# A linear-attention and MLP kernel on one core: row tables made by turning, four stages at once from stage 12 on, and a program listed anew

## The chip, the core and the metric

The kernel runs on one core of a Trainium2 chip. A core has a matrix engine (TensorE, "PE" in the profile), two elementwise engines that read its result banks (VectorE, "DVE", and ScalarE, "ACT"), a general engine (GpSimd, "POOL") and a queue engine (SyncE, "SP"). Each engine takes its instructions in order; they wait for each other through semaphores. The metric is device time in microseconds for one launch, the median of several runs; lower is better.

## What is computed

For 4 batches and 8 heads, 768 tokens of 48 channels each, a decayed linear attention is run along the tokens; its output, 3072 rows of 384, goes through an MLP of 384 to 2048 to 384 with a leaky ReLU:

```python
for t in range(S):
    kt, vt, rt = (k[:, :, t].copy(), v[:, :, t].copy(), r[:, :, t].copy())
    cur = np.einsum('bhd,bhe->bhde', u[None] * kt, vt)
    y[:, :, t] = np.einsum('bhd,bhde->bhe', rt, state + cur)
    state = w[None, :, :, None] * state + np.einsum('bhd,bhe->bhde', kt, vt)
...
h = x @ w_in
g = np.maximum(0.01 * h, h)
return (g @ w_out).astype(np.float32)
```

Inputs and output are fp32 in device memory; the kernel works in bf16 with fp32 accumulation.

## The kernel before

**Stages.** The tokens are cut into 24 stages of 128 tokens of one batch (stage n is batch n mod 4, chunk n div 4), so stage n takes the state that stage n - 4 left. A stage consists of steps, each with a letter in the program:

- `k`, `r`, `v` (`load_one`, L224): three loads, issued by Pool, each 128 x 384, turned to bf16 on the way.
- `P` (`prep_half`, L373, DVE): r times a table of w to the power t, and k times a table of w to the power -t. The tables are the row tables `qtab` and `ktab` (tokens along partitions, channels along a row).
- Turning, so that channels lie along partitions: `T` on PE with a copy `t` on ACT or DVE for stages 0 to 5, `X` (L378) as a DMA transpose on SP's queue from stage 6 on. Stage 0 is turned raw and multiplied with a table that is already turned (`turned`, made by `E`, L337, from w laid along partitions).
- `A` (L465, PE): the 128 x 128 score tiles of eight heads, 8 products into two banks; `M` (`a_mask_half`, L474 and L478, DVE): two masked copies of them into the tile `at`.
- The diagonal with u: for stages 0 to 3 `D`/`Q` scale v (L395); from stage 4 on `q` (`row_sums`, L402, L404, L406, three DVE instructions) makes a sum per token and head, and `Q` (`diag_tile`, L413, two Pool instructions) spreads it onto diagonal tiles in `at`, which the masks of that stage then write into. So a stage's `M` waits for its `A` and for its `Q`.
- `Y` (L604, PE): the stage's output, from `at`, v, the turned r and the state; `y` (L618, ACT) copies it as xT.
- `K` (L506, PE) and `S` (`state`, L569 to L574, DVE): the stage's contribution to the state, and the new state.
- The first MLP product: `G` (`g1`, L643) for one stage, four blocks of 128 hidden channels into one bank by 12 products of 128 columns; `J` (`g1_pair`, L666) for two stages, two blocks by 6 products of 256 columns. `g`, `j` (L653, L676, ACT) empty the bank through the leaky ReLU into gT.
- The second: `H` (`g2`, L690, PE), 16 products of 384 columns for a stage, `h` (L702, ACT) and a store by SP. The last stage's `H` is cut in two.

**Order.** One program is written down and dealt out to the engines, each engine keeping its steps in that order. `Sched.add` notes what each step reads and writes and puts in the waits. The program is a string, `ORDER`, up to about stage 7 (and the first MLP products of stages 0 to 5), and behind it a loop over pairs of stages, m = 3 to 11 (L747): eight `J` of the pair m, with the `A` of the two stages due next inside or behind them, masks, preparation of two stages further on, three loads for each of two stages still further on, row sums and diagonal tiles, one `H` of the pair before, the due `Y`, `K` and `S`, and another `H`. Loads issued in the loop wait until an MLP product of that pair has run (`pace`).

**Banks.** The eight banks of PE's results are handed out in program order, first given back, first taken. A PE step also waits until the bank that it gets has been emptied by whoever had it before.

**Row tables.** `bc` (L318) spreads w over the partitions by two fp32 products, `lnw` (L325) takes its logarithm, and `qtab` and `ktab` (L332) are exponentials of that with the token number as the scale. `F` (L271) are products on a tile of ones that fill PE's time.

Of the kernel before, what the change touches and what calls it, by code (L numbers as in the profile page):

```python
# [24 lines left out]
FIRST, NB, PACE = 6, B, 3  # L25
TURNED, DIAG, CARRY, EXACT, RAW, VISIT, LATE = 6, 4, 4, 1, 1, 3, 3
ORDER = """
w8 k0 r0 w u8 u one trow ones tcol wlz r1 table tri id8 zr v0y k1 F6 Cw Wl exps id wi1 E v0z c0k@ k3 qk0 F11 T0k bc r3
c0q@ W wu8 t0k u16 T0q v0 lnw Cu t0q U qtab r2 C utab F2 A0 X0 P1q ktab v1 D0 M0a T1q wi3 P1k t1q P0k F6 T1k k2 P3k M0b
t1k F5 T3k v3 P3q F1 A1 t3k X1 Q0 r4 F1 D1 M1b T3q K0 k4 Y0 P2q t3q M1a K1 y0 A3 r5 Q1 T2q S1 G0.1 t2q k5 M3a Y1 g0.1  # L30
X3 wi2 G0.3 M3b y1 wi0 P2k G1.3 g0.3 S0 v2 D3 T2k g1.3 Q3 G1.1 t2k P4q v5 K3 P4k Y3 g1.1 X2 wo1 T4q P5q y3 D2 S3 T4k
t4q T5q v4 q5 G3.1 t4k A2 r6 t5q A4 g3.1 G3.3 wo3 P5k G1.2 M2a g3.3 Q5 M2b G3.2 g1.2 q4 G0.2 g3.2 G0.0 g0.2 k6 K2 g0.0
T5k Q2 G1.0 Q4 S2 t5k Y2 g1.0 A5 y2 G3.0 M5b k7 G2.3 M5a g3.0 M4a G2.2 wo2 g2.3 M4b K4 Y5 wo0 g2.2 S4 Y4 y5 r7 G2.1 P6q
y4 k8 J2.1 g2.1 J2.6 r8 q6 j2.1 J2.5 j2.6 r9 J2.3 j2.5 k9 P7k J2.4 j2.3 P6k J2.7 X6T Q6 j2.4 J2.2 j2.7 G2.0 j2.2 J2.0
g2.0 k10 H1 P7q j2.0 v11 q7 X7T v6 v7 P8k H0 h1 P8q Q7 q8 X8T P9q v8 H3 h0 v10 P9k q9 X9T r11 r10 A6 h3 A7 M6a H2 v9
M7a k11 M7b M6b Q9 K6 Y6 h2 S6 Y7 y6 K7 y7 Q8 K5 S7 S5
"""

# [88 lines left out]
def bass_rwkv5_eagle__then__act_leaky_relu_kernel(  # L127
# [16 lines left out]
    NQK, NTP, NVS, NAT, NT, NX, NG, NO = 6, 6, 6, 6, 10, 3, 3, 4  # L144
# [5 lines left out]
    w_row = SB("w_row", [128, HD // 2], FP32)  # L150
    u_row = SB("u_row", [1, HD], FP32)
    one_row = SB("one_row", [128, 128], FP32)
# [7 lines left out]
    lnw = SB("lnw", [128, HD], FP32)  # L160
# [9 lines left out]
    kexp = SB("kexp", [128, 1], FP32)  # L170
# [14 lines left out]
    xT = [SB(f"xT{i}", [128, NSL, 256]) for i in range(NX)]  # L185
    gT = [SB(f"gT{i}", [128, NFB, 256]) for i in range(NG)]
# [101 lines left out]
    def exponents():  # L288
        add("dve", lambda: V.tensor_scalar(kexp[:, :], tcol[:, :], -1.0, -1.0, ALU.mult, ALU.add),
            R=["tcol"], W=["kexp"])  # L290

# [16 lines left out]
    w_bank = []  # L308

    def spread_w():  # L310
        for half in range(2):
            w_bank.append(take())
        assert w_bank[1][1][1] == w_bank[0][1][1] + 1

        def emit():
            for half in range(2):
                at0 = slice(64 * half, 64 * half + 1)
                last = PE.matmul(w_bank[half][0][:, 0:192], one_row[at0, :], w_row[at0, :], start=True, stop=True)  # L318
            return last

        add("pe", emit, R=["one_row", "w_row"], W=[w_bank[0][1], w_bank[1][1]])

    def log_w():
        i = w_bank[0][1][1]
        add("act", lambda: A.activation(lnw[:, :].rearrange("p (two c) -> p two c", two=2),  # L325
                                        ps_all[:, i:i + 2, 0:192], AF.Ln),
            R=[w_bank[0][1], w_bank[1][1]], W=["lnw"])
        give(w_bank[0][1])
        give(w_bank[1][1])

    def table(dst, exps, name, read):
        add("act", lambda: A.activation(dst[:, :], lnw[:, :], AF.Exp, scale=exps[:, 0:1]),  # L332
            R=["lnw", read], W=[name + "tab"])
# [281 lines left out]
    def y_out(n):  # L615
        ps_y, key = y_bank[n]
        m, half = divmod(n, 2)
        add("act", lambda: A.activation(xT[m % NX][:, :, 128 * half:128 * half + 128],  # L618
                                        ps_y[:, 0:HD].rearrange("p (s t) -> p s t", t=128), AF.Copy),
            R=[key], W=[("xT", m % NX, half)])  # L620
        give(key)
# [12 lines left out]
    def g1(n, grp):  # L634
        ps_g, key = g_bank[n, grp] = take()
        m, half = divmod(n, 2)
        ix, t = m % NX, slice(128 * half, 128 * half + 128)

        def emit():
            for f in range(4):  # L640
                fb = 4 * grp + f
                for s in range(NSL):
                    last = PE.matmul(ps_g[:, 128 * f:128 * f + 128], w_in_sb[:, s, 128 * fb:128 * fb + 128],  # L643
                                     xT[ix][:, s, t], start=s == 0, stop=s == NSL - 1)
            return last

        add("pe", emit, R=[("xT", ix, half), ("win", grp)], W=[key, ("pace", n, grp)])

    def g1_out(n, grp):
        ps_g, key = g_bank[n, grp]  # L650
        m, half = divmod(n, 2)
        ig, t = m % NG, slice(128 * half, 128 * half + 128)
        add("act", lambda: A.activation(gT[ig][:, 4 * grp:4 * grp + 4, t],  # L653
                                        ps_g[:, :].rearrange("p (f t) -> p f t", t=128), AF.Prelu, alpha=0.01),
            R=[key], W=[("gT", ig, half, 2 * grp), ("gT", ig, half, 2 * grp + 1)])
        give(key)

    def g1_pair(m, j):
        ps_g, key = g_bank[m, j, 2] = take()
        ix = m % NX  # L660

        def emit():
            for f in range(2):
                fb = 2 * j + f
                for s in range(NSL):
                    last = PE.matmul(ps_g[:, 256 * f:256 * f + 256], w_in_sb[:, s, 128 * fb:128 * fb + 128],  # L666
                                     xT[ix][:, s, :], start=s == 0, stop=s == NSL - 1)
            return last

        add("pe", emit, R=[("xT", ix, 0), ("xT", ix, 1), ("win", j // 2)],  # L670
            W=[key, ("pace", 2 * m, j), ("pace", 2 * m + 1, j)])

    def g1_pair_out(m, j):
        ps_g, key = g_bank[m, j, 2]
        ig = m % NG
        add("act", lambda: A.activation(gT[ig][:, 2 * j:2 * j + 2, :].rearrange("p f t -> p (f t)"),  # L676
                                        ps_g[:, :], AF.Prelu, alpha=0.01),
            R=[key], W=[("gT", ig, 0, j), ("gT", ig, 1, j)])
        give(key)
# [3 lines left out]
    def g2(n, c0=0, c1=HD):  # L683
        ps_o, key = o_bank[n, c0] = take()
        m, half = divmod(n, 2)
        ig = m % NG

        def emit():
            for s in range(NFB):
                last = PE.matmul(ps_o[:, 0:c1 - c0], gT[ig][:, s, 128 * half:128 * half + 128], w_out_sb[:, s, c0:c1],  # L690
                                 start=s == 0, stop=s == NFB - 1)
            return last

        add("pe", emit, R=[("gT", ig, half, j) for j in range(8)] + [("wout", i) for i in range(4)], W=[key])

    def g2_out(n, c0=0, c1=HD):
# [12 lines left out]
        "w": lambda: add("sp", lambda: SP.dma_start(  # L709
            w_row[0:65:64, :], dram(w, 0, [[HD // 2, 2], [1, HD // 2]])),  # L710
            W=["w_row"], dma="w"),
# [35 lines left out]
    for m in range(FIRST // 2, NST // 2):  # L747
        due, ahead, far = ([n for n in (2 * m + x, 2 * m + x + 1) if n < NST] for x in (2, 4, 6))
        late = m < FIRST // 2 + LATE
        for j in range(8):  # L750
            if j == VISIT and not late:
                for n in due:
                    a_mm(n)
# [90 lines left out]
```

## Time and profile before

| | |
|---|---|
| runs | 169.55, 169.41, 168.74 us; median 169.41 |
| the profiled execution | 169.59 us, span 167.8 us from its first to its last instruction |
| granted TensorE clock | 1.00 |
| memory | 20.45 MB read, 4.72 MB written |
| loads through Pool's queue | 76512 packets, 10.03 MB |
| Pool issues of token loads | 70, each 0.92 to 0.93 us on Pool in the mean |

How to read it: an engine's busy time is the time in which it had an instruction, and PE's ends are modelled, so that a busy PE is not a PE at its peak. A row of a group names the line of the kernel, the engine, the operation, what goes out and in, the count, the busy time and the mean of one in ns, and then the idle time before it with what ended it. In the chain of waits each piece is followed back from the last instruction to what released it. In a table of stretches each engine has its busy time and its count of entries, PEclk is the granted clock.

### The profile page before, as it was taken

The numbers are of one execution on the slowest core, as the hardware profiler recorded it, in microseconds if no ns is written. First come the engines' busy times: TensorE is split into PE (matmuls) and PEld (weight loads), VectorE is DVE, ScalarE is ACT, GpSimd is POOL, SyncE is SP. The second block draws the span as 40 slices with busy tenths as digits, with TensorE's granted clock in tenths as the row PEclk, the third lists the DMA queues.
The fourth block names the chain that finished last, engine by engine and source line by source line (L and its number), as shares of the span: only waits on it lengthen the run. The fifth ranks groups of instructions, "written<-read, shape, count | busy, mean of one in ns | idle before, by whom it ended". The sixth has DMA issues, their size and how long they took to land.

```text
span 167.8 us, 4861 instructions
## 1 busy us (share of the span) xinstructions
PE 162.7 (97%) x2089; PEld 123.1 (73%) x2089; DVE 110.5 (66%) x224; ACT 91.3 (54%) x168; POOL 110.8 (66%) x125
## 2 busy tenths in 40 slices
PE   5999999999999999999999999999999999999994
PEld 4577899996668768668668768678678678668563
DVE  7889696928885597596599998996996805000000
ACT  6944888893127437438437537537437447449221
POOL 8999969999997839939949976966960540000000
DMA  7999999999999995996994997995996111011012
GB/s 109 137 158 153 191 178 157 128 170 147 173 148 200 144 127 154 90 101 172 97 131 139 122 141 147 145 126 117 149 98 152 24 47 51 0 47 51 30 63 96
DMA packets 101267, 20.18 MB, mean 120 GB/s; under 512 B 94459, under 2 KB 101246, under 8 KB 101246
## 3 DMA queue, kind: packets, MB, share of 16 engines
q0 software_dynamic: 76512, 10.03, 95.5%
q1 hardware_dynamic: 23694, 9.65, 30.4%
q8 instruction: 16, 0.26, 0.6%
q10 hardware_dynamic: 1040, 0.20, 0.6%
q14 instruction: 5, 0.04, 0.1%
HBM read 20.45 MB, written 4.72 MB: 150 GB/s over the span
## 4 chain that ended last, share of the span: by engine, by line
PE 90%; POOL 4%; DMA 4%; ACT 1%; issue 0%; POOLq 0%
PE ps L690 38%; PE ps L666 32%; PE ps L643 7%; PE ps L604 6%; DMA v_sb<-in_v_dram 4%; PE ps L465 4%; PE ps L506 2%; POOL r_sb L224 2%; PE ps L436 1%; POOL k_sb L224 1%; ACT xT L618 1%; POOL v_sb L224 1%; POOL w_in_sb L234 0%; PE ps L597 0%; POOL trow L256 0%
## 5 line engine op out<-in xcount | busy, mean ns | idle before, releaser
L690 PE MATMUL ps<-w_out_sb,gT 128*128 128x384 bf16 (+2 forms) x400 | 65.6, 320 | 0.0
L413 POOL TENSOR_TENSOR at<-ident,s_tok 128x512 bf16<-128x512 bf16 x40 | 42.5, 1099 | 20.4 <-DVE s_tok L406 20.4
L666 PE MATMUL ps<-xT,w_in_sb 128*128 128x256 bf16 x480 | 55.1, 273 | 0.2 <-ACT xT L618 0.2
L690 PEld LDWEIGHTS ps<-w_out_sb,gT 128*128 128x128 bf16 x400 | 37.7, 98 | 22.4
L676 ACT ACTIVATE gT<-ps 128x512 bf16<-128x512 f32 x80 | 47.8, 597 | 9.2 <-PE ps L666 4.5
L666 PEld LDWEIGHTS ps<-xT,w_in_sb 128*128 128x128 bf16 x480 | 46.4, 98 | 6.9 <-ACT xT L618 0.3
L702 ACT ACTIVATE out_sb<-ps 128x384 f32<-128x384 f32 (+2 forms) x25 | 11.9, 478 | 55.6 <-PE ps L690 55.6
L478 DVE CAST_PREDICATED at<-mask,ps 128x512 bf16<-128x512 uint16 x40 | 24.8, 685 | 21.5 <-PE ps L465 21.5
L224 POOL DMA_DIRECT2D k_sb<-in_k_dram x23 | 21.5, 934 | 4.2 <-PE ps L666 4.2
L224 POOL DMA_DIRECT2D v_sb<-in_v_dram x24 | 22.0, 922 | 0.0
L224 POOL DMA_DIRECT2D r_sb<-in_r_dram x23 | 21.1, 923 | 0.1
L404 DVE TENSOR_TENSOR rku<-r_sb,ku 128x384 bf16<-128x384 bf16 x20 | 17.1, 856 | 0.7
L643 PE MATMUL ps<-xT,w_in_sb 128*128 128x128 bf16 x192 | 12.8, 224 | 0.0
L373 DVE TENSOR_TENSOR qk<-r_sb,qtab 128x384 bf16<-128x384 bf16 x23 | 10.2, 444 | 3.9 <-DMA r_sb<-in_r_dram 3.9
L574 DVE TENSOR_TENSOR st<-sum_t,wl 128x384 bf16<-128x384 bf16 x16 | 11.7, 730 | 0.5
L643 PEld LDWEIGHTS ps<-xT,w_in_sb 128*128 128x128 bf16 x192 | 11.5, 101 | 0.5
L406 DVE TENSOR_REDUCE s_tok<-rku 128x8 f32<-128x384 bf16 x20 | 11.1, 553 | 0.7
L618 ACT ACTIVATE xT<-ps 128x384 bf16<-128x384 f32 x24 | 10.8, 490 | 1.0 <-PE ps L604 0.8
L653 ACT ACTIVATE gT<-ps 128x512 bf16<-128x512 f32 x16 | 9.6, 599 | 2.7 <-PE ps L643 2.1
L604 PE MATMUL ps<-at,v_sb 128*32 128x128 bf16 x384 | 10.9, 223 | 0.0
L373 DVE TENSOR_TENSOR qk<-k_sb,ktab 128x384 bf16<-128x384 bf16 x23 | 8.8, 387 | 0.8 <-DMA k_sb<-in_k_dram 0.8
L604 PEld LDWEIGHTS ps<-tp,st 128*32 128x32 bf16 x240 | 7.2, 96 | 2.7 <-issue 2.5
(66 smaller groups left out, 122.5 us busy)
## 6 DMA issues: line engine op xcount, KB each, us to landing
out_dram<-out_sb SPq DMA_DIRECT2D x23, 192.0 KB, 2.2
v_sb<-in_v_dram POOLq DMA_DIRECT2D x24, 96.0 KB, 6.5
r_sb<-in_r_dram POOLq DMA_DIRECT2D x23, 96.0 KB, 5.9
k_sb<-in_k_dram POOLq DMA_DIRECT2D x23, 96.0 KB, 6.1
w_in_sb<-in_moe_w_in_dram POOLq DMA_DIRECT2D x4, 384.0 KB, 7.8
w_out_sb<-in_moe_w_out_dram POOLq DMA_DIRECT2D x4, 384.0 KB, 8.3
tp<-qk SPq DMA_TRANSPOSE x18, 5.1
k_f<-in_k_dram ACTq DMA_DIRECT2D x1, 192.0 KB, 2.7
```

The costliest lines, as they stand in the source:

```text
L224: add("pool", lambda: G.dma_start(dst, src), R=pace, W=[(which, n)], dma=f"{which}{n}")
L373: add("dve", lambda: V.tensor_tensor(qk[iq][:, H * half:H * half + H, 0:D], hd(src), hd(tab[:, :]), ALU.mult), R=[(name, n), "qk"[half] + ...
L404: add("dve", lambda: V.tensor_tensor(rku[i2][:, :], r_of(n), ku[i2][:, :], ALU.mult), R=[("r", n), ("ku", i2)], W=[("rku", i2)])
L413: add("pool", lambda hh=hh, s_of=s_of: G.tensor_tensor(at[ia][:, hh, :, :], ident[:, :].unsqueeze(1).to_broadcast([128, NP, 128]), s_of.un ...
L478: add("dve", lambda: V.copy_predicated(at[n % NAT][:, hh, :, :], mask[:, :].bitcast(mybir.dt.uint16).unsqueeze(1).to_broadcast([128, NP, 1 ...
L604: last = PE.matmul(ps_y[32 * q:32 * q + 32, 128 * s:128 * s + 128], a, m, start=not whole and step == 0, stop=step == len(columns[q]) - 1)
L618: add("act", lambda: A.activation(xT[m % NX][:, :, 128 * half:128 * half + 128], ps_y[:, 0:HD].rearrange("p (s t) -> p s t", t=128), AF.Copy),
L643: last = PE.matmul(ps_g[:, 128 * f:128 * f + 128], w_in_sb[:, s, 128 * fb:128 * fb + 128], xT[ix][:, s, t], start=s == 0, stop=s == NSL - 1)
L666: last = PE.matmul(ps_g[:, 256 * f:256 * f + 256], w_in_sb[:, s, 128 * fb:128 * fb + 128], xT[ix][:, s, :], start=s == 0, stop=s == NSL - 1)
L676: add("act", lambda: A.activation(gT[ig][:, 2 * j:2 * j + 2, :].rearrange("p f t -> p (f t)"), ps_g[:, :], AF.Prelu, alpha=0.01), R=[key], ...
L690: last = PE.matmul(ps_o[:, 0:c1 - c0], gT[ig][:, s, 128 * half:128 * half + 128], w_out_sb[:, s, c0:c1], start=s == 0, stop=s == NFB - 1)
L702: add("act", lambda: A.activation(out_sb[io][:, c0:c1], ps_o[:, 0:c1 - c0], AF.Copy), R=[key], W=held)
```

## The change

- **Row tables.** `bc`, `lnw`, and the two exponentials go, and with them the load of w as a row, `one_row` and the exponents. In their place the table that stage 0 needs anyway (`turned`) is turned by PE, four products of 128 columns for each half (`TK`, `TQ`), and copied by ACT out of the bank.
- **MLP groups.** `g1`, `g1_pair` and their copies become one function with a width. `Z` takes four stages and one block of 128 hidden channels, 3 products of 512 columns into one bank. Stages 0 to 3 use `G`, 4 to 11 use `J` (so far from 4 on and up to 23), 12 to 23 use `Z`. xT and gT become two buffers of 512 tokens each (so far three of 256).
- **The program.** The loop goes; all steps are in the string, up to the last but one `H`. Stages 12 to 15, 16 to 19 and 20 to 23 have their `Y` one after the other ahead of the `Z` of those four. Loads carry no `pace` any more; they are issued where the string has them. The first loads on Pool are k2, w_in quarter 3, r2, k1, r1, v0, k3, k4, v1, v2, k5, r5, r3 (before: r1, k1, w_in quarter 1, k3, r3, v0, r2, v1, w_in quarter 3, k2). There are 15 filling products (before 32).

```diff
-FIRST, NB, PACE = 6, B, 3
-TURNED, DIAG, CARRY, EXACT, RAW, VISIT, LATE = 6, 4, 4, 1, 1, 3, 3
+NB = B
+TURNED, DIAG, CARRY, EXACT, RAW = 6, 4, 4, 1, 1
...
+w8 v0z v0y trow tcol k0 id k2 ones F2 zr id8 Cw table Wl wi3 r0 wlz u8 F13 wu8 qk0 Cu C c0k T0k tri E t0k c0q TK ktab
+T0q TQ t0q r2 X0 P2k qtab P2q k1 A0 M0a D0 T2k T2q P1k u u16 r1 P1q t2k U v0 t2q T1k t1k T1q t1q M0b Q0 A2 X2 Y0 A1 D2
+k3 M2b k4 v1 P3k M2a y0 W X1 G0.3 v2 K2 Q2 M1a D1 Y2 k5 M1b Q1 Y1 T3k r5 P5q T5q P5k T5k S2 r3 P3q T3q y2 G2.3 utab q5
...
+j5.0 J5.1 J5.4 k19 v15 P17q h6 j5.1 r19 j4.5 v19 K12 X12T q14 S10 Q13 J5.7 j5.7 K13 S13 j5.4 K14 S14 q17 J5.5 P16q J5.6
+K11 j5.2 j5.5 J5.3 j5.3 j5.6 P16k H8 P19q S12 Q14 A13 M13b M13a X15T A14 H9 h8 k18 P17k H11 X16T r18 A12 M14a Q12 X17T
+S11 Q15 Q17 h9 v16 h11 M14b q16 P18k A15 M15b P19k M12a H10 Y13 y13 r20 M12b Y12 y12 Y14 X19T y14 M15a Y15 k20 y15 P18q
+q18 v18 X18T A17 M17b h10 Q16 A16 Q18 M16b K16 M16a K15 S16 Z3.6 Z3.9 Z3.0 Z3.14 q19 Z3.5 P20k z3.0 z3.14 Z3.2 z3.5
...
+Z5.8 z5.8 H16 z5.9 H21 H20 h16 h21 h20 H22 h22
...
-    NQK, NTP, NVS, NAT, NT, NX, NG, NO = 6, 6, 6, 6, 10, 3, 3, 4
+    NQK, NTP, NVS, NAT, NT, NX, NG, NO = 6, 6, 6, 6, 10, 2, 2, 4
...
-    xT = [SB(f"xT{i}", [128, NSL, 256]) for i in range(NX)]
-    gT = [SB(f"gT{i}", [128, NFB, 256]) for i in range(NG)]
+    xT = [SB(f"xT{i}", [128, NSL, 512]) for i in range(NX)]
+    gT = [SB(f"gT{i}", [128, NFB, 512]) for i in range(NG)]
...
+    def turn_table(half):
+        ps_t, key = table_bank[half] = take()
+
+        def emit():
+            for p in range(NP):
+                last = PE.matmul(ps_t[:, 128 * p:128 * p + 128], turned[:, NP * half + p, :], ident[:, :],
+                                 start=True, stop=True)
+            return last
+
+        add("pe", emit, R=["ident"] + [("turned", p) for p in range(NP)], W=[key])
...
+    def g1_wide(n0, width, fb0, count):
+        ps_g, key = g_bank[n0, width, fb0] = take()
+        ix, slots = n0 // 4 % NX, range(n0 % 4, n0 % 4 + width)
+        t, step = slice(128 * slots[0], 128 * slots[0] + 128 * width), 128 * width
+
+        def emit():
+            for f in range(count):
+                fb = fb0 + f
                 for s in range(NSL):
-                    last = PE.matmul(ps_g[:, 128 * f:128 * f + 128], w_in_sb[:, s, 128 * fb:128 * fb + 128],
+                    last = PE.matmul(ps_g[:, step * f:step * f + step], w_in_sb[:, s, 128 * fb:128 * fb + 128],
                                      xT[ix][:, s, t], start=s == 0, stop=s == NSL - 1)
             return last
...
+        "G": lambda n, x: g1_wide(n, 1, 4 * int(x[1:]), 4), "g": lambda n, x: g1_wide_out(n, 1, 4 * int(x[1:]), 4),
+        "J": lambda n, x: g1_wide(2 * n, 2, 2 * int(x[1:]), 2), "j": lambda n, x: g1_wide_out(2 * n, 2, 2 * int(x[1:]), 2),
+        "Z": lambda n, x: g1_wide(4 * n, 4, int(x[1:]), 1), "z": lambda n, x: g1_wide_out(4 * n, 4, int(x[1:]), 1),
```

More of the change, by code (lines that the diff above doesn't have):

```diff
@@ L616, in y_out @@
         ps_y, key = y_bank[n]
[L617 to L618 removed]
+        ix, slot = n // 4 % NX, n % 4
+        add("act", lambda: A.activation(xT[ix][:, :, 128 * slot:128 * slot + 128],
                                         ps_y[:, 0:HD].rearrange("p (s t) -> p s t", t=128), AF.Copy),
[L620 removed]
+            R=[key], W=[("xT", ix, slot)])
         give(key)
@@ L658, in g1_pair @@
[L658 to L671, printed above, removed]
@@ L740, in bass_rwkv5_eagle__then__act_leaky_relu_kernel, with run @@
     }
[L741 to L783 removed]
+    def run(names):
+        for name in names.split():
+            if name in single:
+                single[name]()
+            else:
+                what, n, rest = re.match(r"([A-Za-z]+?)(\d+)(.*)$", name).groups()
+                stage[what](int(n), rest)
+    run(ORDER)
     for c0, c1 in ((0, 256), (256, HD)):
```

150 lines of the change are left out of this document (44 added, 106 removed).

## The prediction

> **What bounds the kernel now.** I read the page's busy shares first, then the chain that ended last in order of time, and then who waits for whom.
>
> ```profile
> span 167.8 us, 4861 instructions
> ...
> PE 162.7 (97%) x2089; PEld 123.1 (73%) x2089; DVE 110.5 (66%) x224; ACT 91.3 (54%) x168; POOL 110.8 (66%) x125
> ```
>
> PE is busy for 97%; apart from its own weight loads nothing is over 66%. The chain (start, length, what) says where the rest is:
>
> ```profile
> 7.58 6.63 DMA v_sb<-in_v_dram
> ...
> 15.84 1.12 PE ps L643 x12
> ...
> 18.98 0.08 PE ps L493 x4
> 19.06 0.24 PE ps L436 x4
> 19.31 0.67 PE ps L643 x12
> 19.98 0.17 PE ps L506 x4
> 20.15 0.17 PE ps L597 x3
> 20.32 0.34 PE ps L604 x16
> ...
> 38.02 7.80 PE ps L690 x48
> 45.82 0.55 PE ps L465 x16
> ...
> 49.80 0.89 ACT xT L618 x2
> ...
> 149.76 5.24 PE ps L666 x48
> 155.00 10.45 PE ps L690 x80
> ```
>
> Until 14.2 us (7.58 + 6.63) the chain waits for the v of stage 1. From there to 165.45 (155.00 + 10.45) it is PE's own work, but for one piece of 0.89 us, where the first paired products wait until ACT has copied two stages' xT. The other engines wait for PE:
>
> ```profile
> DVE at L478 <- PE ps L465: 21.5, 9, 6.4
> ```
>
> So three things can gain: fewer PE microseconds, the 0.89, and the start. What can lose is the path of the masks (DVE and Pool), if the new list uses up these 21.5 us of lead.
>
> **The change part by part.** *512-column products.* Stages 12 to 23 had 6 x 48 = 288 products of 256 columns and get 144 of 512. One of 256 costs 5.24/48 = 109.2 ns, one of 384 costs 7.80/48 = 162.5 ns. Between them lie 0.417 ns a column and 2.5 ns fixed, so 512 columns cost 215.9 ns against 218.4 for two of 256: 144 x 2.5 ns = 0.36 us. Bounds: 0 (512 at the price of two halves) and -0.36; I take -0.36, since both rows lie on one line with a fixed part. What empties the banks must keep up: a group of three such products is 0.647 us of PE, and ACT does three copies of 128 x 512 in 1.57, 0.52 each, a fifth to spare:
>
> ```profile
> 21.09 1.57 ACT L454 ACTIVATE tp<-ps 128x512 bf16<-128x512 f32 x3
> ```
>
> *The 0.89 at 49.8.* In the new list Y6 and Y7 are followed by A9, A8 and K8 (0.55 + 0.17 = 0.72 us) before the first product that reads their xT. The four-stage visits put A17, A16, K16, K15 there (0.9), the last one two groups of stages 16 to 19 (1.3); of the four copies only the last is late. I take -0.89; bounds -0.89 and 0.
>
> *Places of A, K and Y among the products:* the same kinds and counts at other places, so 0; a change of kind costs some hundredths, bounds -0.3 and +0.3.
>
> *Row tables, fills and the start.* The two fp32 spreading products, a logarithm and two exponentials go; eight 128-column products and two copies come; 32 filling products become 15. All lie ahead of PE's dense stretch, where the loads cover them; uncovered, the eight would be two pieces like the 0.24 at 19.06. The loads decide the start:
>
> ```profile
> 1.41 1.06 POOL L224 DMA_DIRECT2D r_sb<-in_r_dram  x1
> 2.46 0.90 POOL L224 DMA_DIRECT2D k_sb<-in_k_dram  x1
> 3.33 0.77 POOL L234 DMA_DIRECT2D w_in_sb<-in_moe_w_in_dram  x1
> ```
>
> These are issues on Pool; the list of DMAs, asked for the stretch of each issue, gives the time to landing as its last number:
>
> ```profile
> r_sb<-in_r_dram POOLq DMA_DIRECT2D x1, 96.0 KB, 4.0
> k_sb<-in_k_dram POOLq DMA_DIRECT2D x1, 96.0 KB, 4.3
> ```
>
> ```profile
> w_in_sb<-in_moe_w_in_dram POOLq DMA_DIRECT2D x1, 384.0 KB, 6.4
> ```
>
> They land at 5.4, 6.8 and 9.7. Two later ones:
>
> ```profile
> 8.45 0.80 POOL L234 DMA_DIRECT2D w_in_sb<-in_moe_w_in_dram  x1
> 9.18 0.97 POOL L224 DMA_DIRECT2D k_sb<-in_k_dram  x1
> ```
>
> ```profile
> w_in_sb<-in_moe_w_in_dram POOLq DMA_DIRECT2D x1, 384.0 KB, 7.7
> k_sb<-in_k_dram POOLq DMA_DIRECT2D x1, 96.0 KB, 7.6
> ```
>
> These land at 16.15 and 16.8. Loads land one after the other: a quarter of w_in takes 2.9 (9.7 - 6.8) or 1.95 (16.15 less the 14.2 of v ahead of it), a token load 0.65 (16.8 - 16.15) to 0.9 (the five between 9.7 and 14.2). The new order on Pool is k2, w_in 3, r2, k1, r1, v0, k3, k4, v1, v2, k5, r5, r3. With 2.9 and 0.73, k2 lands at 5.4, w_in at 8.3, v0 at 11.2, v2 at 14.1, r3 at 16.3. Behind v2 the DVE has, in its order, the scaled v of stage 2, two masks, the scaled v of stage 1 (some 2.4 us together, counted with 0.6 each), then two halves of stage 5, a state and a half of stage 3 (1.4). So Y1 starts on PE at 16.5 and the last turning of stage 3 ends at 18.2; from there the list is dense. By 18.2 PE has done ten turnings (0.24 each), three A (0.28), three D (0.08), one K (0.17), three Y (0.51) and one G (0.67), 5.8 us. The chain of before, counted in the same way, had seven turnings, three A, two D, two K, two Y and two G by then, 5.4. As walked, the start is 0.4 better.
>
> Against it stands PE's rate. The 12 products at 15.84 took 1.12 us and the 12 at 19.31 took 0.67: early ones run at little over half speed. If that lasts until 20 or 22 us in place of 17, it costs up to 2.1 more. So the start lies between -1.35 (the quarter of w_in at 1.95) and +1.7. I take 0: nearer to the walk, with part of the slow rate paid.
>
> The Trainium skill, "TensorE: Matmul & The Clock Gate", Part 1, says that the array runs at half its clock until a window of about 3.4 us has been busy. The two rows agree, and the rule speaks against dropping fills: counted from Y1 at 16.5 the full rate would come at 19.9 at the earliest.
>
> *New waits.* A visit of four stages needs eight masks and four pairs of Pool's diagonal tiles. A DVE instruction with both operands in SBUF stretches when it meets such a tile (the first row has the durations as least, median and most):
>
> ```profile
> L404 DVE TENSOR_TENSOR rku<-r_sb,ku x20: 357/358/2910, 21.6 to 132.0; 128x384 bf16<-128x384 bf16 x20
> ```
>
> ```profile
> 95.92 2.33 DVE L404 TENSOR_TENSOR rku<-r_sb,ku 128x384 bf16<-128x384 bf16 x1
> 95.92 2.10 POOL L413 TENSOR_TENSOR at<-ident,s_tok 128x512 bf16<-128x512 bf16 x2
> ```
>
> So a pass of two stages costs the DVE (its busy time is the fourth number) less or more, at the same 20 entries of its timeline:
>
> ```profile
> 75.80:88.24 12.44, 12.44 (x162) 9.25 (x161) 9.22 (x20) 6.61 (x12) 9.58 (x11) 1.00 1.30 131
> ```
>
> ```profile
> 100.68:113.12 12.44, 12.44 (x162) 9.24 (x161) 11.52 (x20) 6.61 (x12) 9.96 (x11) 1.00 1.52 141
> ```
>
> Between the masks of stage 4 and those of stage 15 the new list has 63 us of PE work and about six passes' worth for the DVE: 55 us at 9.22, 69 at 11.52. The tightest place is M12 and M15 ahead of Y12 and Y15. Walked with hardly a stretch, the last mask there is 0.5 us early; with a stretch at each meeting it is 2.3 late; with a DVE that never idles at 11.52 a pass, 5.6 late. Three smaller places (a half of stage 12 ahead of K12, a state ahead of the bank of a product, the masks of stage 5 ahead of a bank) come to half a microsecond each and go into the same delay, since PE's being late gives the DVE time. I take +0.2, near the early end: the part of the old program that was listed by hand, as all of it is now, meets no stretch between 28 and 40 us,
>
> ```profile
> L404 DVE TENSOR_TENSOR rku<-r_sb,ku 128x384 bf16<-128x384 bf16 x2 | 0.7, 358 | 0.1
> ```
>
> and the loops do, between 100 and 135:
>
> ```profile
> L404 DVE TENSOR_TENSOR rku<-r_sb,ku 128x384 bf16<-128x384 bf16 x6 | 8.0, 1328 | 0.2
> ```
>
> *The end.* Eight output products (20.8 us) and the sixteen last groups (10.4) follow the last Y, so nothing behind them waits for masks; the last product, copy and store are as before: 0.
>
> **Sum.** -0.36 - 0.89 + 0 + 0 + 0.2 = -1.05. The profiled execution took 169.59 us around its span of 167.8, 0.18 above the median of the runs. 169.59 - 1.05 = 168.54 there, and with the same 0.18 off about 168.3 as a median.
>
> **The rivals.** *The masks come late (slower).* At the joint visit of stages 12 to 15 the DVE is behind, because its SBUF instructions stretched under Pool's tiles, and PE waits at Y12 and Y15. For it: the 2.33 row and the 11.52 pass; against it: 21.5 us of lead now and the unstretched 358 ns. It decides from about 0.8 us of stretch for each pair of tiles. Price: 2.3 as walked, 3.3 with the smaller places ahead of it; with 2.8 in place of 0.2 the time is 169.41 - 1.25 + 2.8 = 171.0. The Trainium skill, "SBUF — State Buffer", Who interferes with whom, says that these two engines share ports which the first one holds for a whole instruction while the other stands still; the 2.33 beside two of Pool's tiles is more than one hold.
>
> *The start eats it (no change).* PE stays slow until 20 to 22 us, or token loads land at 0.9 each. Start +1.7: 169.41 - 1.25 + 1.7 + 0.2 = 170.1. For it: the 1.12 row and the idle time ahead of Y1; against it: the old list had gaps too and was at speed by 19 us. By the clock gate's rule alone, with 3.4 us at half speed from 16.5, the start would be about +0.7 and the time 169.1.
>
> *All fits (faster still).* The quarter of w_in at 1.95, no stretch: start -1.35, waits 0: 169.41 - 1.25 - 1.35 = 166.8.
>
> *It does not do what it says.* If 512 columns cost what two of 256 do, only 0.36 is lost: 168.7, within the forecast's own range.
>
> **How the numbers follow.** Forecast 0.42 (own range 167.4 to 168.9), late masks 0.25, start 0.18, all fits 0.15. A measurement of this kernel can tell about 0.5% from no change, so faster is below 168.56 and slower above 170.26. Faster: 0.36 of the forecast and all of "all fits", 0.51. Same: 0.06 of the forecast, 0.14 of the start, 0.04 of late masks, 0.24. Slower: 0.21 and 0.04, 0.25. The range for 8 in 10 goes from 166.5 (all fits, with the places at their better bound) to 171.2 (late masks at 3.0).
>
> **What would show it.** Right: products of 512 columns at about 216 ns each; no ACT xT piece in the chain behind 40 us; PE dense from about 18 us and idle under 0.5 us behind 30. Late masks: PE idle ahead of Y12 or Y15, at 90 to 96 us, ended by a mask on DVE, with rku over 1 us before it. The start: 12 products of 128 columns still at 1.1 us past 19 us. Wrong altogether: PE idle in the last 35 us, or ACT ending PE's waits in the groups of four.

## The result, and the profile after

The changed kernel takes 175.65 us (median of four runs, 175.34 to 176.05) against 169.48 for the kernel before beside it: a ratio of 1.037, 95% interval 1.0324 to 1.0415. Forecast were 168.3 and a range of 166.5 to 171.2. The profiled execution took 175.91, of which 173.9 are its span.

The page of the changed kernel, its span and busy shares:

```profile
span 173.9 us, 4547 instructions
...
PE 161.0 (93%) x1926; PEld 108.2 (62%) x1932; DVE 114.3 (66%) x221; ACT 83.3 (48%) x168; POOL 111.1 (64%) x125
```

PE is busy for 1.7 us less than before and the span is 6.1 longer. So PE does not do more: it waits. Who makes it wait (total, times, longest), in the view of waits of the changed kernel, behind the filling products of the start:

```profile
PE ps L672 <- DVE sum_t L577: 3.4, 1, 3.4
...
PE ps L441 <- DVE qk L378: 1.4, 2, 1.2
```

Both of these waits end with DVE. And where DVE waited 21.5 us for the scores of PE before, it now waits less than half of that:

```profile
DVE at L483 <- PE ps L470: 9.8, 5, 4.7
```

The chain that ended last (start, length, what) shows two stretches in which DVE, not PE, sets the pace:

```profile
19.18 1.37 DVE qk L378 x2
...
21.58 1.26 DVE prod L393
...
23.90 1.21 DVE at L479 x2
...
39.95 7.80 PE ps L672 x48
...
69.93 1.29 DVE at L483 x2
...
83.60 3.69 DVE ku L407
...
87.31 1.09 DVE rku L409
...
91.57 0.48 DVE sum_t L577
...
92.10 4.06 PE ps L672 x16
```

The first lies at the start, 19 to 25 us. The second runs from 69.93 to 92.05 with nothing but DVE in it. At its end PE's second product of stage 11 (`H11`, L672) gets the bank from which DVE takes the new state of stage 12 (`S12`, the sum at 91.57), and DVE reaches `S12` late. Behind `H11` PE's queue holds the scores of stages 12 and 15, `H10` and the four `Y`, so everything shifts. The chain has no piece for the xT copies any more, which had cost 0.89 at 49.8, and PE does not wait for masks at `Y12` and `Y15` (`Y12` starts at 100.00, 0.08 after the last product before it). In e5 below it does.

Why DVE is late is in its timeline. Of the changed kernel, DVE, Pool and PE in turn (start, length, instructions; in brackets the idle time before and what ended it):

```profile
83.53 3.75 DVE L407 TENSOR_TENSOR ku<-k_sb,u_tab 128x384 bf16<-128x384 bf16 x1
...
83.99 4.18 POOL L418 TENSOR_TENSOR at<-ident,s_tok 128x512 bf16<-128x512 bf16 x4
...
92.10 4.06 PE L672 MATMUL ps<-w_out_sb,gT 128*128 128x384 bf16 x16 [3.36 <-DVE sum_t L577]
```

The product of k and u of stage 17, 0.35 us when nothing disturbs it, takes 3.75: it ends at 87.28, just behind the third of four of Pool's diagonal tiles (83.99 + 3 x 1.045 = 87.1; spans on Pool are rough). The tiles are those of stages 12 and 15. The third row shows a second loss: the sixteen products of `H11` take 4.06 us where sixteen take 2.60 elsewhere. The table of stretches explains it (length, busy time of PE, PEld, DVE, ACT and POOL with entries, granted clock, DMA share, GB/s):

```profile
90.00:92.00 2.00, 0.00 (x0) 0.00 (x0) 2.00 (x3) 0.00 (x0) 2.00 (x3) 0.83 0.17 40
92.00:94.00 2.00, 1.90 (x7) 0.89 (x8) 1.97 (x6) 0.00 (x0) 2.00 (x4) 0.50 1.19 132
94.00:96.00 2.00, 2.00 (x11) 1.04 (x9) 1.97 (x5) 0.00 (x0) 0.88 (x2) 0.81 1.79 94
96.00:98.00 2.00, 2.00 (x26) 1.29 (x26) 1.86 (x5) 0.49 (x1) 0.65 (x1) 1.00 1.72 173
```

After 3.36 us without work PE is granted half its clock until about 95. So the visit costs 3.36 + (4.06 - 2.60) = 4.82 us in the trace. The second part is no cause of its own: e5 shows a run without it that is no faster.

How full DVE is before that point, over the same 26 us in the kernel before and in the changed one (the columns as above):

```profile
66.00:92.00 26.00, 26.00 (x342) 19.27 (x341) 19.56 (x42) 13.66 (x25) 20.30 (x22) 1.00 1.25 118
```

```profile
66.00:92.00 26.00, 22.73 (x249) 15.79 (x246) 25.20 (x39) 9.56 (x20) 23.43 (x25) 0.99 1.56 140
```

DVE has 6.4 us to spare in the old list and 0.8 in the new one.

### The profile page after: what moved, and what is told of

It is laid out like the page before. It is cut to its first block, busy times and chain, and to the rows that moved or that the text cites. A ratio compares the mean times of both kernels' runs of the same rounds, so it can differ in the third digit from the quotient of the medians.

```text
span 173.9 us, 4547 instructions
## 1 busy us (share of the span) xinstructions
PE 161.0 (93%) x1926; PEld 108.2 (62%) x1932; DVE 114.3 (66%) x221; ACT 83.3 (48%) x168; POOL 111.1 (64%) x125
## 4 chain that ended last, share of the span: by engine, by line
PE 69%; DVE 15%; POOL 7%; DMA 3%; issue 2%; ACT 2%; DVEq 0%; POOLq 0%
PE ps L672 31%; PE ps L648 29%; PE ps L609 5%; DVE qk L378 4%; DMA r_sb<-in_r_dram 3%; PE ps L470 3%; POOL k_sb L237 3%; DVE ku L407 3%; POOL r_sb L237 2%; POOL v_sb L237 2%; ACT gT L659 1%; DVE at L483 1%; DVE st L579 1%; DVE sum_t L577 1%; PE ps L511 1%
## 5 line engine op out<-in xcount | busy, mean ns | idle before, releaser
L672 PE MATMUL ps<-w_out_sb,gT 128*128 128x384 bf16 (+2 forms) x400 | 66.6, 324 | 3.4 <-DVE sum_t L577 3.4
L648 PE MATMUL ps<-xT,w_in_sb 128*128 128x128 bf16 (+2 forms) x522 | 66.5, 283 | 1.3 <-DVE tp L457 0.5
L659 ACT ACTIVATE gT<-ps 128x512 bf16<-128x512 f32 x96 | 51.2, 605 | 24.6 <-PE ps L648 24.1
L672 PEld LDWEIGHTS ps<-w_out_sb,gT 128*128 128x128 bf16 x400 | 38.4, 99 | 28.7 <-DVE sum_t L577 3.8
L648 PEld LDWEIGHTS ps<-xT,w_in_sb 128*128 128x128 bf16 x528 | 43.3, 99 | 18.8 <-DVE tp L457 0.7
L378 DVE TENSOR_TENSOR qk<-r_sb,qtab 128x384 bf16<-128x384 bf16 x23 | 15.0, 659 | 2.8 <-DMA r_sb<-in_r_dram 2.8
L407 DVE TENSOR_TENSOR ku<-k_sb,u_tab 128x384 bf16<-128x384 bf16 x20 | 12.9, 646 | 0.0
L577 DVE TENSOR_TENSOR sum_t<-ps,st 128x384 bf16<-128x384 f32 x16 | 8.8, 550 | 5.4 <-PE ps L511 5.1
L409 DVE TENSOR_TENSOR rku<-r_sb,ku 128x384 bf16<-128x384 bf16 x20 | 10.1, 503 | 0.7
L470 PE MATMUL ps<-tp 48*128 48x128 bf16 x192 | 8.6, 228 | 1.5 <-issue 0.8
L579 DVE TENSOR_TENSOR st<-sum_t,wl 128x384 bf16<-128x384 bf16 x16 | 9.2, 575 | 0.6
L609 PEld LDWEIGHTS ps<-at,v_sb 128*32 128x32 bf16 x384 | 8.9, 99 | 0.6 <-issue 0.4
```

Source lines behind the costliest of these rows:

```text
L378: add("dve", lambda: V.tensor_tensor(qk[iq][:, H * half:H * half + H, 0:D], hd(src), hd(tab[:, :]), ALU.mult), R=[(name, n), "qk"[half] + ...
L407: add("dve", lambda: V.tensor_tensor(ku[i2][:, :], k_of(n), u_tab[:, :], ALU.mult), R=[("k", n), "u_tab"], W=[("ku", i2)])
L470: last = PE.matmul(at_bank[n][hh][0][:, 128 * p:128 * p + 128], tp[it][rows, NP + p, :], tp[it][rows, p, :], start=True, stop=True)
L609: last = PE.matmul(ps_y[32 * q:32 * q + 32, 128 * s:128 * s + 128], a, m, start=not whole and step == 0, stop=step == len(columns[q]) - 1)
L648: last = PE.matmul(ps_g[:, step * f:step * f + step], w_in_sb[:, s, 128 * fb:128 * fb + 128], xT[ix][:, s, t], start=s == 0, stop=s == NSL ...
L659: add("act", lambda: A.activation(gT[ig][:, fb0:fb0 + count, t], ps_g[:, :].rearrange("p (f t) -> p f t", t=128 * width), AF.Prelu, alpha= ...
```

## The experiments

My theory: DVE's instructions with two operands in SBUF stretch under Pool's diagonal tiles. The old list had room for that, the new one has not. Rivals: the list itself is too tight for DVE even unstretched; one badly placed step is to blame; Pool's length is to blame; PE's clock at the start. Where nothing else is named, the kernel that is edited is the changed one.

**e1: all tiles filled without a read.** The u term of stages 4 to 23 is left out.

```diff
-            add("pool", lambda hh=hh, s_of=s_of: G.tensor_tensor(
-                at[ia][:, hh, :, :], ident[:, :].unsqueeze(1).to_broadcast([128, NP, 128]),
-                s_of.unsqueeze(2).to_broadcast([128, NP, 128]), ALU.mult),
+            add("pool", lambda hh=hh, s_of=s_of: G.memset(at[ia][:, hh, :, :], 0.0),
```

> Pool's diagonal tiles (40 tensor operations that read two SBUF tiles) are replaced by 40 fills with zero that read nothing; the u term of stages 4 to 23 is left out. Theory (stretch): DVE instructions with two SBUF operands stand still while Pool is in a diagonal tile, and this list puts them ahead of something that PE needs at two places: ku of stage 17 (3.75 us where 0.35 is its bare time) ahead of S12 and the bank of H11, and P4q, P4k, prod3 (1.05, 1.50, 1.26 us) ahead of T4k. Then all these fall to 0.3 to 0.45 us, the 3.4 us that PE waits ahead of H11 goes with the slow 1.46 us behind it, and about 2 of the start: 167.5 to 170. Rival (too much on the DVE, or a list whose order is late by itself): the DVE is late anyway, 174 to 176, with the same wait at H11.

Measured: 169.01, ratio to the kernel before 0.997 (0.9952 to 0.9987). Its page:

```profile
PE 159.4 (96%) x1926; PEld 107.8 (65%) x1932; DVE 91.5 (55%) x221; ACT 83.0 (50%) x168; POOL 87.1 (52%) x125
```

DVE executes the same 221 instructions in 91.5 us in place of 114.3. So 22.8 us of its busy time were stretch, and without the stretch the new list loses nothing: 6.6 us come back. But Pool became shorter as well, 111.1 to 87.1; e8 separates the two.

**e2: the state of stage 12 earlier in the list.**

```diff
-K13 S13 j5.4 K14 S14 q17 J5.5 P16q J5.6 ... P16k H8 P19q S12 Q14 A13
+K13 S13 j5.4 K14 S14 S12 q17 J5.5 P16q J5.6 ... P16k H8 P19q Q14 A13
```

> Only the state of stage 12 moves, from behind q17, P16 and P19q to right behind the state of stage 14 on DVE; PE's banks follow (A13 gets the bank of S12, H11 that of a copy on ACT). Theory (stretch, and a bank held by a late DVE step): H11 no longer waits; the masks of stage 13, still behind the stretched ku, then hold A12's banks for 1 to 2 us: 172 to 174. Rival (the state was only the messenger: all of the wait moves to the masks): 175 to 176, PE waiting about 3.4 us ahead of A12.

Measured: 176.3, ratio 1.0389 (1.0329 to 1.045), no gain. In its chain the long piece is another instruction, the one that now stands there, and behind it DVE goes on to the masks:

```profile
85.36 3.17 DVE st L579
...
93.22 1.20 DVE at L483 x2
```

The wait of `H11` is gone from its waits, and others stand in its place:

```profile
PE ps L470 <- DVE at L483: 2.4, 2, 1.9
PE ps L609 <- DVE at L483: 1.7, 1, 1.7
```

So the place of `S12` is not the cause. DVE owes a whole visit's work, and whichever step PE asks for first shows the debt.

**e3: the tiles of stage 12 earlier**, behind their row sums, so that those of stage 15 stand alone.

```diff
-H4 S6 J4.2 q12 A10 P13k A11 ... A12 M14a Q12 X17T
+H4 S6 J4.2 q12 Q12 A10 P13k A11 ... A12 M14a X17T
```

> Only Pool's diagonal tile of stage 12 moves, from in front of that of stage 15 to right behind its row sums, so that at 84 us one pair of tile operations runs and not two in a row (4.18 us). Theory (stretch): ku of stage 17 takes 2.2 us at most and not 3.75, PE's wait ahead of H11 falls from 3.4 to 1.5 to 2.0, and with it part of the slow stretch behind: 172.5 to 174.5. Rival (the DVE is late for another reason): 175 to 176, same wait.

Measured: 175.46, ratio 1.0363 (1.0311 to 1.0415). I had looked for more. Its chain:

```profile
70.31 1.54 issue
...
86.02 1.69 DVE ku L407
```

The instruction at the visit is down to 1.69, but a half of stage 13's preparation now stands still at 70.31 (that piece of "issue" is within one DVE instruction of 2.62). Pool now has four tiles in a row there, from 67.38 to 71.71. PE waits 1.6 us ahead of `H11` and 1.3 for the masks ahead of `Y12`. The stretch moved; it did not become less (DVE is busy for 114.6 us, 114.3 in the changed kernel).

**e4: the tiles of stage 5 later**, behind the loads of w_out.

```diff
-g1.3 D3 K1 Q3 v4 Q5 t4q v5 K3 ... A4 wo0 wo3 A5
+g1.3 D3 K1 Q3 v4 t4q v5 K3 ... A4 wo0 wo3 Q5 A5
```

> Only Pool's diagonal tile of stage 5 moves, from behind the load v4 (20.3 us) to behind v5, k6 and two quarters of w_out (about 24 us). Theory (stretch): P4q, P4k and prod3 take 0.35, 0.3 and 0.42 us and not 1.05, 1.50 and 1.26, and PE's three waits between 20.4 and 25.2 us (1.24, 0.49, 0.25) shrink by 1.5 or more: 173.5 to 174.5. Rival (the load r4, landed at 19.16, and not the stretch sets this place): change under 0.5, 175.2 to 176.

Measured: 175.02, ratio 1.0342 (1.0299 to 1.0385), less of a gain than I had expected. The waits at the start are gone, that of `H11` is 3.4 as before. The chain:

```profile
38.48 7.80 PE ps L672 x48
...
90.64 5.30 PE ps L672 x16
```

1.47 us are won by 39.95. `H11` starts 1.46 earlier, but its products take 5.30 in place of 4.06, since the half clock lasts longer there. In that trace 0.2 remains by the end of `H11`.

**e5: 512-column products cut into halves.**

```diff
-                for s in range(NSL):
-                    last = PE.matmul(ps_g[:, step * f:step * f + step], w_in_sb[:, s, 128 * fb:128 * fb + 128],
-                                     xT[ix][:, s, t], start=s == 0, stop=s == NSL - 1)
+                part = min(step, 256)
+                for c in range(0, step, part):
+                    for s in range(NSL):
+                        last = PE.matmul(ps_g[:, step * f + c:step * f + c + part],
+                                         w_in_sb[:, s, 128 * fb:128 * fb + 128],
+                                         xT[ix][:, s, t.start + c:t.start + c + part], start=s == 0, stop=s == NSL - 1)
```

> Every 512-column product of Z is made as two of 256 columns into the same bank; all else as in the changed kernel. By the prediction's term 144 more products cost 2.5 ns each, 0.36 us in all, and this part of the PE's work is paid in full since it lies behind the stretch where PE waits: 175.65 + 0.4, so 175.8 to 176.3. Rival (512 columns cost what two halves do, or more): 175.65 or less.

Measured: 175.53, ratio 1.0341 (1.0317 to 1.0364), on the rival's side of the changed kernel's 175.65, but a time cannot resolve 0.36 us there. The chains can. Nine products of 512 in the changed kernel, then the same columns in eighteen here:

```profile
125.40 1.94 PE ps L648 x9
```

```profile
124.75 1.96 PE ps L650 x18
```

215.6 ns for 512 columns and 217.8 for two of 256: 2.2 ns saved, near the 2.5 forecast. The rows are rounded to 0.01 us, so the 2.2 is good to about 1 ns.

This run shows something else. PE waits 3.36 us ahead of `H11`, just as in the changed kernel, but here the granted clock stays at 1.00 and the sixteen products take no longer than usual:

```profile
92.24 2.77 PE L675 MATMUL ps<-w_out_sb,gT 128*128 128x384 bf16 x16 [3.36 <-DVE sum_t L577]
```

(The same view gives 2.77 for the next sixteen of the changed kernel and 4.06 for `H11`.) Yet nothing is gained, since PE then waits 1.36 us for the masks ahead of `Y12`. From the start of `H11` to that of `Y12` it is 7.90 us in both runs (92.10 to 100.00, and 92.24 to 100.14). In e5 DVE's way from `S12` to the masks of stage 12 sets it; in the changed kernel the slow products fill the same time.

**e6: the whole visit relieved, with the computation complete.** ACT writes the tiles of stages 12, 15 and 17, identity times the row sum as a scaled copy; the tiles of stage 5 are late as in e4; those of 12, 15 and 17 stand behind `h7`, `j5.6` and `h8`.

```diff
+        if n in (12, 15, 17):
+            for hh in range(2):
+                for p in range(NP):
+                    add("act", lambda hh=hh, p=p: A.activation(
+                        at[ia][:, hh, p, :], ident[:, :], AF.Copy,
+                        scale=s_tok[n % 4][:, 2 * p + hh:2 * p + hh + 1]),
+                        R=["ident", ("s", n % 4)], W=[("at", ia, hh)])
+            return
```

> Pool's tile of stage 5 late as in e4; the diagonal tiles of stages 12, 15 and 17 are written by ACT (eight scaled copies of the identity each) at places where ACT was idle. Theory (from 66 to 92 us the DVE is the bound, and it is so because a quarter of its time is stretch under Pool's tiles): without those three pairs its two-operand instructions run bare between 82 and 89 us, the wait ahead of H11 (3.4) and the slow products behind it (1.46) go, and the start gains 1.4: 169.5 to 171.5. Rival (any relief at one place is taken back at the next mask, as in e2 and e3): 174 to 175.5.

Measured: 168.65, ratio 0.9962 (0.9936 to 0.9987). Its timeline, DVE and ACT:

```profile
81.74 0.35 DVE L407 TENSOR_TENSOR ku<-k_sb,u_tab 128x384 bf16<-128x384 bf16 x1
...
83.32 0.35 DVE L378 TENSOR_TENSOR qk<-k_sb,ktab 128x384 bf16<-128x384 bf16 x1
...
82.38 2.44 ACT L419 ACTIVATE at<-ident,s_tok 128x128 bf16<-128x128 bf16 x8
```

The same product that stood for 3.75 us takes 0.35. It ends before the eight ACT tiles shown, but the preparation at 83.32, which runs beside them, takes 0.35 as well (1.23 at 89.23 in the changed kernel, beside Pool's tiles). The reader of the identity is now an engine that does not hold DVE up, and the new list is 7.0 us better for it (with the later tiles of stage 5), more than I had expected.

**e7: only the tiles of stages 12, 13, 14, 15 and 17 filled without a read** (their u term is left out).

```diff
+            if n in (12, 13, 14, 15, 17):
+                add("pool", lambda hh=hh: G.memset(at[ia][:, hh, :, :], 0.0),
+                    R=["ident", ("s", n % 4)], W=[("at", ia, hh)])
+                continue
```

> Only the tiles of stages 12, 13, 14, 15 and 17 are filled with zero without reading (their u term is left out); the other 15 stages keep Pool's tensor operations. Theory: the stretch between 74 and 92 us alone makes the wait ahead of H11; it goes, the start's waits (20 to 25 us) stay, so of e1's 6.6 about 4.5 to 5 come back: 170.5 to 171.5. Rival (the stretch is spread, and the DVE is late from before 74 us): 172.5 to 174.5.

Measured: 171.18, ratio 1.0076 (1.0048 to 1.0104). The visit's share is 175.65 - 171.18 = 4.5, against 4.8 read from the trace. The waits of the start are still there.

**e8: every tile filled twice, without a read.** The u term of stages 4 to 23 is left out; Pool stays as long as it was.

```diff
+            for again in range(2):
+                add("pool", lambda hh=hh: G.memset(at[ia][:, hh, :, :], 0.0),
+                    R=["ident", ("s", n % 4)] + [("at", ia, hh)] * again, W=[("at", ia, hh)])
```

> As e1 (all tiles filled with zero without reading, the u term of stages 4 to 23 left out), but each filled twice in a row, so that Pool is occupied for about as long as with its tensor operation (2 x 0.54 us beside 1.10). It parts the stretch on DVE from Pool's own length. Theory (the read of two SBUF tiles by both engines is what costs): DVE instructions stay at 0.35 us and the time stays near e1's, 168.5 to 170.5. Rival (Pool's tiles being late is what costs): 173 to 176, with masks waiting for Pool.

Measured: 168.67, ratio 0.9947 (0.9923 to 0.997). Its page, and the stretch before the visit:

```profile
PE 159.2 (95%) x1932; PEld 107.5 (64%) x1932; DVE 91.2 (55%) x221; ACT 83.2 (50%) x168; POOL 108.1 (65%) x165
```

```profile
66.00:92.00 26.00, 26.00 (x282) 17.93 (x280) 21.08 (x51) 9.53 (x19) 24.46 (x39) 1.00 1.75 158
```

Pool is as busy as in the changed kernel (108.1 against 111.1), and DVE is as quick as in e1. So what stretches DVE is Pool's operation that reads, not that Pool is busy, writes, or delivers late. DVE's bare work between 66 and 92 us is 21.1 of 26: the list is full but feasible. That rules out a list too tight by itself. The same can be read between two fixed points. From the masks of stage 11 to the sum in `S12` DVE takes 22.1 us in the changed kernel (69.93 to 92.05) and 15.1 here (68.16 to 83.23). PE has 18.9 us of its own work over that stretch (69.87 to 88.74), so it waits in the one and not in the other.

By the Trainium skill, "SBUF — State Buffer", Who interferes with whom, a DVE instruction with two inputs in SBUF contends with a GpSimd instruction that reads SBUF and not with one that only writes it. The pages of e1 and e8 agree: 91.5 and 91.2 against 114.3.

**b1: the kernel before, all tiles filled without a read** (the u term of stages 4 to 23 is left out), with the edit of e1.

> The kernel before, with all 40 of Pool's tiles filled with zero without reading (the u term of stages 4 to 23 is left out). Theory (the old list has the same stretch, but leaves the DVE so much spare time that PE never waits for it): its DVE busy time falls from 110.5 to 92 or less, and the time stays, 169.0 to 169.8. In the stretch from 66 to 92 us its bare DVE work is then well below the 21.1 us that the new list has there (e8), about 15 to 17. Rival (the stretch costs the old list too, so that it is not the new order that makes it matter): 164 to 167.

Measured: 169.31, ratio 0.9996 (0.9965 to 1.0026). Its page and the same stretch:

```profile
PE 161.7 (97%) x2089; PEld 121.9 (73%) x2089; DVE 91.7 (55%) x224; ACT 91.4 (55%) x168; POOL 87.6 (52%) x125
```

```profile
66.00:92.00 26.00, 26.00 (x343) 19.26 (x341) 17.93 (x43) 13.62 (x26) 15.58 (x22) 1.00 1.30 125
```

The old list carried 110.5 - 91.7 = 18.8 us of the same stretch and paid nothing for it. In it DVE has 17.9 us of bare work in these 26, more than the 15 to 17 that I had expected; the new list has 21.1 (43 and 51 entries).

**e9: e6 without its filling products** (`F2` and `F13` are taken out of the string).

> e6_act_tiles without any filling product (15 fewer). The prediction had a rival in which fewer fills leave PE at half rate until 20 to 22 us. In the changed kernel's trace the rate was full from 16.4 us on with 15 fills. Theory (the dense work from 10 us on raises the rate, not the fills): time as e6, 168.2 to 169.2, 36 products of 128 columns in about 2.2 us at 18 us. Rival (the fills do it): the early products at 107 ns each past 18 us, 169.7 to 171.

Measured: 168.07, ratio 0.9943 (0.9913 to 0.9973), the fastest version here; the intervals of e6 and e9 overlap. In both, the first twelve products of the MLP take 1.44 us (at 14.03 here, at 13.88 in e6). And the 48 products that began at 39.95 in the changed kernel begin at the same time in both, at 38.33 in e6 and 38.30 in e9. So these 15 fills do not buy PE's rate at the start.

**e10: only the tiles of stages 4 to 7 filled without a read** (their u term is left out), with the edit of e7.

> The changed kernel with the tiles of stages 4 to 7 filled by a memset that reads nothing (their u term is left out), all others as they are. My theory: what the bare visit left of the loss is the start, where tiles of stage 5 hold the DVE between 19 and 25 us. Taking the stretch away there brings the 48 products that began at 39.95 to about 38.0, and as PE and DVE both come earlier, the time falls by 1.5 to 2.0, to 173.6 to 174.2; the wait of product H11 for the DVE stays at about 3.4. Rival: the DVE's work between 28 and 90 us is one chain that a quicker start does not shorten, as the later place of Q5 suggested with its 0.6; then the wait of H11 grows by what the start gains, to 5, and the time is 175.0 or more.

Measured: 173.44 (172.59 to 174.39), ratio 1.0237 (1.0163 to 1.031): just below the range of my theory, which the wait of `H11` bears out too. Chain and waits:

```profile
37.99 7.80 PE ps L676 x48
...
90.25 5.30 PE ps L676 x16
```

```profile
PE ps L676 <- DVE sum_t L581: 3.5, 1, 3.5
```

The start's share is 39.95 - 37.99 = 1.96 in the trace and 175.65 - 173.44 = 2.2 in the time. Together with the visit's 4.5 that makes 6.7, and e1 gave back 6.6: the two places account for about the whole loss. The agreement is closer than the numbers are: the four runs of e10 are two of 172.59, one of 174.3 and one of 174.39, so the start's share is known to about 1 us.

**e11: only the tiles of stages 8 to 11 filled without a read** (their u term is left out).

> The changed kernel with the tiles of stages 8 to 11 filled without a read (their u term is left out), all others as they are. My theory: the DVE's chain that makes H11 late starts at about 70 us, when the scores of two stages have just been made by PE, so what the DVE saves before 70 is lost in waiting there: H11's wait stays at 3 or more and the time within 0.5 of the changed kernel, 175.2 to 176.1. Rival: the lateness is gathered over the whole list, so that each stage's unstretched tiles give their share: four of them against the five of the visit give 3 or more, a time of 172.7 or less and a wait of H11 under 1.

Measured: 174.51, ratio 1.0321 (1.0268 to 1.0373), between the two expectations. The chain stays on PE until 79.77, not 69.87, so what DVE saves earlier does reach the visit; but the last ten microseconds ahead of `H11` alone make a wait of 2.3, and the masks another:

```profile
PE ps L676 <- DVE sum_t L581: 2.3, 1, 2.3
PE ps L613 <- DVE at L487: 1.4, 1, 1.4
```

I had been wrong that savings before 70 us are lost. How much of the 1.1 us gained is more than scatter cannot be said: the interval overlaps with that of the changed kernel.

## Why the prediction was wrong

*The step that failed is "New waits", taken at +0.2.* By e1 and e8 it measures 175.65 - 169.01 = 6.6 to 175.65 - 168.67 = 7.0, of which about 4.5 stand at the visit (e7) and about 2 at the start (e10). Everything else in the sum together was forecast as -1.25; e1 and e8 give 0.997 and 0.9947 of 169.5, that is -0.5 and -0.9, with the right sign and somewhat less.

*The mechanism was named, as a rival, and its size was not.* DVE's SBUF instructions stretch under Pool's tiles, and PE waits. It was priced at 2.8 and given 0.25. The forecast stood on three readings that do not carry:
- The 358 ns between 28 and 40 us of the old list were taken for "listed by hand" in general. The row holds two instructions. The one pair of tiles in that stretch fell into 3.85 us in which DVE waited for a load, and the next pair (at 40.32) met an instruction, still in the part listed by hand, just behind the stretch that was read:

```profile
34.77 2.12 POOL L413 TENSOR_TENSOR at<-ident,s_tok 128x512 bf16<-128x512 bf16 x2
...
40.11 2.52 DVE L373 TENSOR_TENSOR qk<-r_sb,qtab 128x384 bf16<-128x384 bf16 x1
```

  In the new list, all written by hand, the products of k and u take 646 ns in the mean and those with r 503, where 384 and 856 had been the old list's. So listing by hand did not take the stretch away; it put it on other instructions:

```profile
L407 DVE TENSOR_TENSOR ku<-k_sb,u_tab 128x384 bf16<-128x384 bf16 x20 | 12.9, 646 | 0.0
...
L409 DVE TENSOR_TENSOR rku<-r_sb,ku 128x384 bf16<-128x384 bf16 x20 | 10.1, 503 | 0.7
```

- "21.5 us of lead" is a sum over nine waits in the whole span. What can absorb stretch is the spare time in the stretch ahead of one deadline: 6.4 us of 26 in the old list, and by e8 4.9 in the new one even without stretch. This could have been worked out before: count each list's DVE instructions between two points of PE's work.
- The largest stretch of a pass seen before was 11.52 - 9.22 = 2.3, though the prediction's own row of `rku` had one instruction of 2910 ns. The old list, too, had four tiles in a row (at 47.59 and 61.48), but they did not cost PE a wait. In the new list four in a row, at 83.99, met a product of k and u that stands ahead of `S12`, and that instruction alone lost 3.4.

*The place was only half right.* `Y12` and `Y15` were named. PE stops earlier, at `H11`, for a bank. A state ahead of the bank of a product was listed among the "smaller places" of half a microsecond. e2 shows that the two are one debt: without the wait at `H11` the masks take it over. And in e5 PE waits at both, 3.36 us at `H11` and 1.36 at `Y12`; in the changed kernel the slow products of `H11` cover the second wait.

*Two terms were missing.* The start was walked with loads and with PE's rate, but without a stretch of DVE; the tiles of stages 4 to 7 cost 1.96 to 2.2 there (e10), those of stage 5 most of it (1.47, e4). And no wait was priced with a slower clock behind it. Behind `H11` that is 1.46 us in the changed kernel, where it cost nothing extra (e5), and 2.7 in e4 and e10, where it did: in e10 PE takes 10.49 us from `H11` to the scores behind the `Y` of stage 15 (90.25 to 100.74), in the changed kernel 9.25 (92.10 to 101.35).

*What was right.* The 512-column products save 2.2 ns each (e5; 2.5 forecast). The xT wait is gone. The end is unchanged and ACT keeps up (its longest hold on a `Z` is 0.2). PE's slow rate did not last until 20 to 22 us: 36 products of 128 columns from 17.97 on take 60 ns each, so that rival falls:

```profile
17.97 2.17 PE L648 MATMUL ps<-xT,w_in_sb 128*128 128x128 bf16 x36
```

Whether PE's clock made the early products slow is not shown: the granted clock is 1.00 in every stretch of both starts, while twelve products took 1.12 us at 15.84 before and take 1.44 at 13.93 now.

That the start of loads and fills was taken as 0 fits e8, which has the new loads and fills: its 48 products begin at 38.01, those of the kernel before at 38.02.

## What to carry to other kernels

A lead summed over a span is no reserve: ahead of each point at which the bounding engine would wait, compare the other engine's work, stretch included, with the time it has. A stretch that costs nothing in one order (b1) costs nearly 4% in another with nearly the same instructions, and moving the step that shows the wait (e2, e3) does not pay the debt; taking away its cause does (e6: another engine writes the tiles). An idle time of the matrix engine can bring a slower rate behind it, which is to be priced only where the engine would not have had to wait there anyway (e5).

## What the runs showed of the hardware

A DVE instruction can stand across several of Pool's reading tiles that follow each other, though each tile is an instruction of 1.05 us: 3.75 us across three here and 3.17 in e2. It is not always so: the first instruction was let in between the third and the fourth tile, and the next one (`rku`, 1.09 us at 87.31) stood only across the fourth. What decides this is not shown.

A wait of about 3.4 us can halve PE's clock, and need not. It did in the changed kernel (3.36), in e4 (3.37) and in e10 (3.47), and it did not in e5 (3.36). After the 2.34 us of e11 the clock stayed at 1.00. The windows of e10 and of e11, each with the end of PE's idle time in its second row:

```profile
88.00:90.00 2.00, 0.00 (x0) 0.00 (x0) 2.00 (x3) 0.00 (x0) 2.00 (x3) 0.81 0.07 17
90.00:92.00 2.00, 1.75 (x6) 0.87 (x7) 1.97 (x6) 0.00 (x0) 2.00 (x3) 0.50 1.14 147
92.00:94.00 2.00, 2.00 (x8) 0.88 (x6) 1.97 (x5) 0.00 (x0) 1.02 (x2) 0.50 1.65 84
94.00:96.00 2.00, 2.00 (x17) 0.96 (x17) 1.55 (x5) 0.35 (x1) 0.49 (x1) 0.50 1.57 163
96.00:98.00 2.00, 2.00 (x21) 1.25 (x18) 1.53 (x3) 0.14 (x1) 1.59 (x2) 0.99 1.44 249
```

```profile
88.00:90.00 2.00, 0.00 (x0) 0.00 (x0) 2.00 (x3) 0.49 (x1) 2.00 (x3) 1.00 0.07 16
90.00:92.00 2.00, 1.74 (x11) 1.09 (x12) 1.97 (x6) 0.00 (x0) 2.00 (x3) 1.00 1.12 147
```

How long the half clock held follows from the rows: a row of 2 us at clock c has 4 x (1 - c) us of it. In the changed kernel that is 0.68 + 2 + 0.76 = 3.4, in e10 0.76 + 2 + 2 + 2 + 0.04 = 6.8, just twice as much. The length of the wait does not decide between the two: e4, with the changed kernel's wait, has 6.8 as well. That is how e4 and e10 lose at `H11` 1.2 us of what they win at the start. The half clock also begins inside the wait: in the changed kernel at 92.00 - 0.68 = 91.32, 2.6 us after PE stopped at 88.74, and in e10 at 89.24, 2.5 us after it stopped at 86.78.

By the Trainium skill, "TensorE: Matmul & The Clock Gate", Part 1, an idle window of about 3.4 us brings the half clock, a busy one ends it, and the windows run freely. The two durations, 3.4 and 6.8, agree with one and two such windows, and equal waits with different outcomes (the changed kernel and e5) agree with windows that run freely, without testing it. One thing differs: the half clock began 2.5 to 2.6 us after PE's last product, so a window of 3.4 us that ended there was not idle throughout.
